# Three moves in the issue order of one tuned kernel: a gate step, a block's first sums, and one half's outputs

## The chip, the cores and the metric

The kernel runs on one core of a Trainium2 chip. The time is device time of one execution in microseconds (us), given as the median of several runs; lower is better. The core has TensorE (PE, matrix products; its weight loads are listed as PEld), VectorE (DVE), ScalarE (ACT), GpSimd (POOL) and SyncE (SP, which issues the transfers).

## The reference

Attention with a window and a few sink positions over 2 x 8 heads of 768 positions, then a mixture of 8 experts, then a feed-forward layer with a squared ReLU:

```python
x = attention(q, k, v)                      # 1536 tokens x 512
P = exp(x @ w_gate - max)                   # 1536 x 8
for _ in range(8):
    P /= P.sum(1) + 1e-9
    P /= P.sum(0) + 1e-9
    P *= N / E
for e in range(8):
    out += P[:, e] * (relu(out_of_attention @ w1[e]) @ w2[e])
h = relu(out @ w_in); result = (h * h) @ w_out
```

All of it is asked for in fp32. The kernel splits every operand of a product into a high and a low part (names that end in h and l) and adds three products: high by high, high by low, low by high.

## The kernel before

**Chunks.** The experts' weights are cut into 16 chunks of 512 hidden columns (c = 0 to 15, two for an expert), the last layer into four (c = 16 to 19). Each chunk has a first product (x by w1 to hidden units h) and a second (h by w2, added up in `acc`). The 1536 tokens are handled as three blocks of 512: blocks 0 and 1 together, and the third block (number 2) alone.

**Fast chunks.** `is_fast` (c = 2 to 15 and 17 to 19) computes first products with a Strassen-like scheme of seven products p1 to p7 on quarters of the operands (`fast`, line 818). Each pi is six matmuls on TensorE (`products`), and an ei behind it takes its result out of PSUM and adds it up on VectorE and ScalarE. It runs with q = 0 on blocks 0 and 1 (512 columns), and with q = 1 on the third block (256 columns), each time for two halves of the hidden units, which I call first half and second half.

**The third block.** With q = 1 a half has only four PSUM banks, a to d, and two groups of products. The first group fills p1 in a, p6 in b, p5 in c, p7 in d (24 matmuls). The second group adds p2 to a, p3 to c, p4 to d (18 matmuls). So p2 may start only when e1 has copied a, p3 only when e5 has read c, p4 only when e7 has read d. The sums hang together: e1 copies a on ACT (tile `txs`), e6 adds it to b (`tu`), e5 adds that to c (the first `tx`), e7 adds that to d (the second `tx`).

The list that `fast` returns is unpacked as `(a, b, *e)` for the first half and `(f, g, *i)` for the second: a and f are the first groups, b and g the second groups, e[0] to e[6] are e1 to e7, and i[0] to i[6] are the same of the second half (I write i1 to i7 for them).

**Outputs.** e2, e3, e4 and e7 hand a result to `to_h` (line 765). For c >= 16 that is a ReLU on ACT (L770), a product on DVE (L771), a copy to `hh` on ACT (L782), and a subtraction to `hl` on DVE (L783). The last two are put in a queue that the next `finish()` issues. For c < 16 it is a ReLU to `hh` on ACT (L767), and `hl` on DVE (L777).

**Order.** Each engine takes its instructions in the order of the program text. `run` goes through `seq`, a list of groups of matmuls, and after group k issues what `plan[k]` holds; `put(m + k, step)` puts a step behind group m + k, where m is the first group after the products of blocks 0 and 1. For 17 <= c the groups from m on are: a, the four second-product groups of block 1 (`second(c, 1)`, 12 matmuls of 512 columns each, at L946, and behind each an addition to `acc` on DVE, L683 or L690), b, f, g, and then `second(c, 0)`. For c < 16 they are the four groups of `second(c, 1)`, a, b, f, g.

**The gate.** `gate` (line 986) computes P. It is a generator: `run` advances it behind those groups whose running number stands in `GATE_AT`. Each of its eight iterations sums rows on DVE and scales (L1024 to L1026), and after a `yield` sums columns by one product with a matrix of ones on TensorE (L1031), whose result DVE uses (L1035 to L1041). The last advance issues the last of these products; it falls into chunk c = 2.

Of the kernel before, what the change touches and what calls it, by code (L numbers as in the profile page):

```python
# [36 lines left out]
FAST, FAST2 = 2, NC1 + 1  # L37
NC = NC1 + NC2
CONV = 3
CONV_AT = (0, 1, 2, 3, 8, 9, 10, 11, 12, 13, 14, 15)  # L40
GATE_AT = (0, 1, 2, 3, 5, 7, 9, 11, 13, 16, 19, 22, 25, 28)
W2_AT = (2, 5, 8, 11)
NB = 512
BIG = 1e30
# [4 lines left out]
class Kernel:  # L49
# [780 lines left out]
    def fast(self, c, half, q):  # L830

        nc = self.nc
        v = {}
        UNITS = {"A11": 0, "A12": 1, "A22": 3, "S2": 4, "S4": 5, "S3": 6, "S1": 7}
        w = NB >> q

        def at(i, f):
            return (c, 2, f, slice(w * i, w * i + w)) if q else (c, i, f, slice(0, w))

        f0, f1 = 2 * half, 2 * half + 1  # L840

        def mul(bank, a, b):
            first = bank not in v
            if first:
                v[bank] = self.mmtile()[:, 0:w]
            self.products(
                v[bank], [(self.weight(c, half, UNITS[a]), self.operand(b, q))], start=first
            )

        def scr(tag):  # L850
            if not q:
                return self.scratch2(tag)
            if (c, tag) not in self.third:
                self.third[c, tag] = self.scratch2(tag)
            return self.third[c, tag][:, w * half : w * half + w]

        def tt(name, a, b, tag=None):
            v[name] = v[b] if tag is None else scr(tag)
            nc.vector.tensor_tensor(out=v[name], in0=v[a], in1=v[b], op=ALU.add)  # L859

        def out(i, f, src):
            c, t, f, s = at(i, f)
            self.to_h(c, t, f, v[src], s)

        def p1():
            mul("a", "A11", "B11")

        def e1():
            if half == 0:
                for t in (2,) if q else (0, 1):  # L870
                    self.h_tiles(c, t)
            v["s"] = self.scratch2("xs" if q else "x0", w)
            nc.scalar.activation(out=v["s"], in_=v["a"], func=AF.Copy)  # L873
            self.finish()

        def p6():
            mul("b", "S2", "T2")

        def e6():
            tt("u", "b", "s", "u")  # L880
            self.finish()

        def p5():
            mul("c", "S1", "T1")

        def e5():
            tt("z", "c", "u", "x0")
            self.finish()

        def p2():  # L890
            mul("a", "A12", "B21")

        def e2():
            self.finish()
            out(0, f0, "a")

        def p7():
            mul("d", "S3", "T3")

        def e7():  # L900
            tt("c22", "d", "z", "x2")
            self.finish()
            out(1, f1, "c22")

        def p3():
            mul("c", "S4", "B22")

        def e3():
            tt("c12", "c", "u", "x0")
            self.finish()  # L910
            out(1, f0, "c12")

        def p4():
            mul("d", "A22", "T4")

        def e4():
            tt("c21", "d", "u")
            self.finish()
            out(0, f1, "c21")

        def chain(*steps):
            def go():
                for step in steps:
                    step()
            return go

        if q == 0:
            pairs = (p1, e1), (p6, e6), (p5, e5), (p2, e2), (p7, e7), (p3, e3), (p4, e4)
            return [chain(*pair) for pair in pairs]
        return chain(p1, p6, p5, p7), chain(p2, p3, p4), e1, e2, e3, e4, e5, e6, e7  # L930

    def second(self, c, t):
# [394 lines left out]
    def phase_b(self, c0, first, fill):  # L1327
# [44 lines left out]
        def run(seq, plan):  # L1372

            for k, g in enumerate(seq):
                g()
                for step in plan.get(k, ()):
                    step()
                if next(groups) in GATE_AT:
                    next(gate, None)
# [5 lines left out]
        for c in range(c0, NC):  # L1385
            if c == 2:
                self.steps = conv
            plan = {}

            def put(k, *step):  # L1390
                plan.setdefault(k, []).append(partial(*step))

            off = 0
            if not low:
                run([self.plain(c, 1, 0), *rest], {})
                low = first.close() or True
                self.w2p = self.pool(left, "w2" + n)
                self.tp = self.pool(left, "T" + n)
                self.cp, self.T = self.pool(left, "c" + n), {}
                seq = [self.plain(c, t, f) for t in (1, 0) for f in range(KD)][1:]  # L1400
            elif self.is_fast(c):
                seq = self.fast(c, 0, 0) + self.fast(c, 1, 0)
            else:
                seq = [self.plain(c, t, f) for t in (1, 0) for f in range(KD)]
            for k in range(4):
                put(W2_AT[k] if self.is_fast(c) else k, self.part_w2, c, k)
            if c == NC1:
                x = [self.x2(2, kc) for kc in range(KD)]
                seq = sum(([s, *x[k : k + 1]] for k, s in enumerate(seq)), [])
            m = len(seq)  # L1410
            if self.is_fast(c):
                (a, b, *e), (f, g, *i) = (self.fast(c, half, 1) for half in range(2))
                if c < FAST2:
                    seq += self.second(c, 1) + [a, b, f, g]
                else:
                    seq += [a] + self.second(c, 1) + [b, f, g]
                for k, step in (
                    (4, e[0]), (4, e[5]), (4, e[4]), (4, e[6]),
                    (6, i[0]), (6, e[1]), (6, e[2]), (6, i[5]), (6, i[4]), (6, e[3]), (6, i[6]),
                    (7, i[1]), (7, i[2]), (7, i[3]),  # L1420
                ):
                    put(m + k, step)
            else:
                seq = seq + self.second(c, 1) + [self.plain(c, 2, f) for f in range(KD)]
            if c == NC1 - 1:
                x = [self.x2(t, kc) for t in (1, 0) for kc in range(KD)]
                seq += sum(
                    ([s, x[k]] for k, s in enumerate(self.second(c, 0) + self.second(c, 2))), []
                )
                wide = lambda k: m + k if k < 8 else m + 2 * k - 8  # L1430
            else:
                seq += self.second(c, 0) + self.second(c, 2)
                wide = lambda k: m + k
            if c in (FAST - 1, FAST2 - 1):
                t = self.sums(0)
                for k in range(13):
                    put(k if c < FAST else min(2 * k, k + 5), next, t, None)
                t = self.sums(1)
                for k in range(13):
                    put(m + 8 + k // 2, next, t, None)  # L1440
            if c + 1 < NC:
                if self.is_fast(c + 1):
                    for half in range(2):
                        for k in range(2):
                            put(wide(2 * half + k), self.unit_sums, c + 1, half, k)
                            put(wide(6 + 2 * half + k), self.units, c + 1, half, 3, k)
                for half in range(2):
                    for k in range(2):
                        put(wide(10 + 3 * half + k), self.units, c + 1, half, 0, k)
            if c > 1:  # L1450
                for k in CONV_AT:
                    put(wide(k), next, conv, None)
                    put(wide(k), next, conv, None)
            run(seq, plan)
# [94 lines left out]
```

## Time and profile before

| | us |
|---|---|
| median of 3 runs | 1413.39 |
| the three runs | 1411.85, 1413.39, 1413.79 |
| the profiled execution's own time | 1413.57 |
| its span, first to last instruction | 1411.7 |
| TensorE busy | 1386.1 |
| VectorE busy | 976.4 |
| POOL busy, ACT busy | 537.3, 471.9 |

The page gives each engine's busy time and share of the span; the list of waits says which engine waited for whom; the timeline gives one row for an instruction (start, duration, engine, source line, operation, output and inputs, shape, and in square brackets how long the engine sat idle before it and what ended that). Matmul rows are pipelined: from one to the next the start moves by less than the duration in the row, so steps are taken from start to start. A line such as L859 is the line of a helper (`tt` of `fast`), so the place is told by the time.

### The profile page before, as it was taken

Reading aid. Unit: us, or ns where it says so; the run is one execution under the profiler, and the core shown is the slowest. Engines: PE = TensorE matmul, PEld = TensorE weight load, DVE = VectorE, ACT = ScalarE, POOL = GpSimd, SP = SyncE. Lnnn points to the kernel's source line nnn. Section 1 sums busy time; section 2 is a strip of 40 time slices with the busy share of each in tenths; the row PEclk is TensorE's granted clock in tenths of the full one; section 3 lists DMA queues with packets and bytes.
Section 4 is the critical chain, followed back from the end, with each engine's and each line's share of the span. In section 5 each row is a group of like instructions: output and inputs, shape, how many; then the busy total and the mean of one; then the engine's idle time right before and its main releaser. Section 6 shows DMA issues by size and latency. Waiting matters only on the chain.

```text
span 1411.7 us, 19345 instructions
## 1 busy us (share of the span) xinstructions
PE 1386.1 (98%) x7225; PEld 1179.8 (84%) x7225; DVE 976.4 (69%) x1932; ACT 471.9 (33%) x1065; POOL 537.3 (38%) x485
## 2 busy tenths in 40 slices
PE   8999999999999999999999999999999999999997
PEld 6888888788888888888888888888888888878786
DVE  7889638888777777777767777765454468846563
ACT  8767423322222222222222222222232243423231
POOL 7534226543442334344233434423342037523210
PEclk9999999999999999999999999999999999999999
DMA  4322110123223232322323232230111010110101
GB/s 161 100 79 88 46 40 30 60 67 105 82 90 105 75 105 68 105 83 90 105 75 105 68 105 83 90 105 31 60 46 60 30 47 27 63 61 30 45 31 63
DMA packets 61148, 102.55 MB, mean 73 GB/s; under 512 B 3956, under 2 KB 43252, under 8 KB 60788
## 3 DMA queue, kind: packets, MB, share of 16 engines
q1 hardware_dynamic: 61040, 101.22, 22.5%
q8 instruction: 59, 0.97, 0.3%
q14 instruction: 45, 0.37, 0.1%
q10 hardware_dynamic: 4, 0.00, 0.0%
HBM read 89.67 MB, written 11.53 MB: 72 GB/s over the span
## 4 chain that ended last, share of the span: by engine, by line
PE 76%; DVE 1%; ACT 0%; issue 0%; ACTq 0%; DVEq 0%
PE mm L946 41%; PE mm L799 35%; PE mm L963 0%; DVE tx L859 0%; ACT hh L782 0%; DVE tu L859 0%; DVE hl L783 0%; DVE acc L690 0%; DVE tx L771 0%; ACT tx L770 0%; DVE tu L771 0%; ACT txs L873 0%; DVE mm L771 0%; DVE acc L686 0%; DVE raw L615 0%
## 5 line engine op out<-in xcount | busy, mean ns | idle before, releaser
L946 PE MATMUL mm<-w2h,hh 128*128 128x512 f32 (+1 forms) x916 | 357.4, 390 | 0.0
L946 PE MATMUL mm<-w2l,hh 128*128 128x512 f32 (+1 forms) x916 | 356.3, 389 | 0.0
L946 PE MATMUL mm<-w2h,hl 128*128 128x512 f32 (+1 forms) x916 | 355.9, 389 | 0.0
L519 POOL TENSOR_TENSOR w2l<-raw,w2h 128x512 fp32r<-128x512 f32 x76 | 118.4, 1557 | 372.1 <-ACT w2h L518 370.1
L690 DVE SCALAR_TENSOR_TENSOR acc<-mm,P,acc 128x512 f32<-128x512 f32 x168 | 125.7, 748 | 137.2 <-PE mm L946 136.0
L946 PEld LDWEIGHTS mm<-w2h,hl 128*128 128x128 f32 x916 | 172.3, 188 | 36.0
L946 PEld LDWEIGHTS mm<-w2h,hh 128*128 128x128 f32 x916 | 172.4, 188 | 34.6
L946 PEld LDWEIGHTS mm<-w2l,hh 128*128 128x128 f32 x916 | 172.4, 188 | 34.4
L562 POOL TENSOR_TENSOR raw<-raw 128x256 f32<-128x256 f32 x136 | 125.7, 928 | 9.1 <-DMA raw<-w 1.0
L519 POOL TENSOR_TENSOR s0l<-raw,s0h 128x512 fp32r<-128x512 f32 (+1 forms) x36 | 45.6, 1266 | 202.5 <-ACT s0h L518 186.8
L767 ACT ACTIVATE hh<-tx 128x512 fp32r<-128x512 f32 (+1 forms) x112 | 58.9, 526 | 90.9 <-DVE tx L859 90.4
L859 DVE TENSOR_TENSOR tx<-mm,tu 128x512 f32<-128x512 f32 (+1 forms) x136 | 75.5, 555 | 17.5 <-PE mm L799 13.6
L859 DVE TENSOR_TENSOR tx<-mm,tx 128x512 f32<-128x512 f32 (+1 forms) x68 | 37.7, 555 | 58.7 <-PE mm L799 57.3
L777 DVE SCALAR_TENSOR_TENSOR hl<-tx,hh 128x512 fp32r<-128x512 f32 (+1 forms) x112 | 69.9, 624 | 7.6 <-ACT hh L767 7.6
L873 ACT ACTIVATE tx<-mm 128x512 f32<-128x512 f32 x34 | 20.4, 599 | 161.3 <-PE mm L799 159.4
L683 DVE TENSOR_TENSOR acc<-mm,acc 128x512 f32<-128x512 f32 (+1 forms) x49 | 33.2, 677 | 58.2 <-PE mm L946 58.1
L873 ACT ACTIVATE txs<-mm 128x256 f32<-128x256 f32 x34 | 13.0, 383 | 173.9 <-PE mm L799 173.9
L767 ACT ACTIVATE hh<-mm 128x512 fp32r<-128x512 f32 (+1 forms) x68 | 34.3, 505 | 102.0 <-PE mm L799 102.0
L519 POOL TENSOR_TENSOR a0l<-raw,a0h 128x512 fp32r<-128x512 f32 (+1 forms) x38 | 43.0, 1149 | 51.8 <-ACT a0h L518 51.8
L519 POOL TENSOR_TENSOR a1l<-raw,a1h 128x512 fp32r<-128x512 f32 (+1 forms) x38 | 40.4, 1084 | 53.3 <-ACT a1h L518 53.3
L799 PE MATMUL mm<-xl,a1h 128*128 128x512 f32 (+1 forms) x172 | 60.3, 350 | 0.0
L799 PE MATMUL mm<-xl,a0h 128*128 128x512 f32 (+1 forms) x172 | 59.8, 348 | 0.0
(276 smaller groups left out, 3409.3 us busy)
## 6 DMA issues: line engine op xcount, KB each, us to landing
raw<-w SPq DMA_DIRECT2D x110, 512.0 KB, 3.6
raw<-win SPq DMA_DIRECT2D x16, 512.0 KB, 4.0
w<-m SPq DMA_DIRECT2D x32, 256.0 KB, 4.5
raw<-wout SPq DMA_DIRECT2D x16, 512.0 KB, 4.1
raw<-qkv SPq DMA_DIRECT2D x8, 624.0 KB, 3.9
raw<-qkv SPq DMA_DIRECT2D x7, 464.0 KB, 3.4
out<-acc SPq DMA_DIRECT2D x11, 256.0 KB, 2.0
wraw<-w SPq DMA_DIRECT2D x2, 1024.0 KB, 5.9
```

Source lines behind the costliest of these rows:

```text
L519: self.nc.gpsimd.tensor_tensor(out=lo, in0=src, in1=hi.bitcast(F32), op=ALU.subtract)
L562: self.nc.gpsimd.tensor_tensor(out=o, in0=x, in1=y, op=op)
L683: nc.vector.tensor_tensor(out=a, in0=ps, in1=a, op=ALU.add)
L690: nc.vector.scalar_tensor_tensor(out=a, in0=ps, scalar=self.P[:, ti, e : e + 1], in1=a, op0=ALU.mult, op1=ALU.add)
L767: nc.scalar.activation(out=hh, in_=src, func=AF.Relu)
L777: nc.vector.scalar_tensor_tensor(out=hl, in0=src, scalar=0.0, in1=hh.bitcast(F32), op0=ALU.max, op1=ALU.subtract,)
L799: self.nc.tensor.matmul(out=ps, lhsT=w[:, kc], rhs=x[:, kc], start=start and k == 0, stop=(k == n - 1), skip_group_check=True,)
L859: nc.vector.tensor_tensor(out=v[name], in0=v[a], in1=v[b], op=ALU.add)
L873: nc.scalar.activation(out=v["s"], in_=v["a"], func=AF.Copy)
L946: self.nc.tensor.matmul(out=ps[:, d], lhsT=x[:, f, s], rhs=w[:, f, d], start=(n == 0), stop=(n == 11),)
```

## The change

The table of the gate has 30 in place of 28 as its last entry. Of the third block's steps, e1, e6 and e5 stand behind group m + 2 in place of m + 4 where c >= 17; e2 and e3 stand behind group b (m + 5) in place of behind f (m + 6); behind f, e4 stands last. The tile for the third block's h is made in e7 in place of e1.

```diff
-GATE_AT = (0, 1, 2, 3, 5, 7, 9, 11, 13, 16, 19, 22, 25, 28)
+GATE_AT = (0, 1, 2, 3, 5, 7, 9, 11, 13, 16, 19, 22, 25, 30)
...
         def e1():
-            if half == 0:
-                for t in (2,) if q else (0, 1):
+            if half == q == 0:
+                for t in (0, 1):
                     self.h_tiles(c, t)
...
         def e7():
             tt("c22", "d", "z", "x2")
+            if half == 0 and q:
+                self.h_tiles(c, 2)
             self.finish()
             out(1, f1, "c22")
...
+                early = 4 if c < FAST2 else 2
                 for k, step in (
-                    (4, e[0]), (4, e[5]), (4, e[4]), (4, e[6]),
-                    (6, i[0]), (6, e[1]), (6, e[2]), (6, i[5]), (6, i[4]), (6, e[3]), (6, i[6]),
+                    (early, e[0]), (early, e[5]), (early, e[4]), (4, e[6]), (5, e[1]), (5, e[2]),
+                    (6, i[0]), (6, i[5]), (6, i[4]), (6, i[6]), (6, e[3]),
                     (7, i[1]), (7, i[2]), (7, i[3]),
                 ):
                     put(m + k, step)
```

**The gate's last product, on TensorE, in chunk c = 2.** The names `mm_` are PSUM tiles; the products are the first half's p6 (T0, s0), p5 (x, s0), p2 (x, a0) and p7 (T0, s0). Before:

```order
L799 MATMUL mm_3321<-T0h_2760,s0h_3072 128x512
L799 MATMUL mm_3321<-T0h_2760,s0l_3073 128x512
L1031 MATMUL mm_3330<-P_84,ones_2508 128x117
L799 MATMUL mm_3335<-xl_82,s0h_3072 128x512
L799 MATMUL mm_3335<-xh_81,s0h_3072 128x512
```

Now, from the middle of p2 on:

```order
L799 MATMUL mm_3308<-xl_82,a0h_3179 128x512
L799 MATMUL mm_3308<-xh_81,a0h_3179 128x512
L799 MATMUL mm_3308<-xh_81,a0l_3180 128x512
L1033 MATMUL mm_3350<-P_84,ones_2508 128x117
L799 MATMUL mm_3355<-T0l_2761,s0h_3072 128x512
L799 MATMUL mm_3355<-T0h_2760,s0h_3072 128x512
```

The product with the ones stood between p6 and p5; now p5 and p2, twelve matmuls, stand ahead of it, and p7 behind it.

**The third block of chunk c = 17, on VectorE.** `acc` rows are the additions behind the groups of `second(c, 1)`; mm_11257, 11264, 11271, 11278 are the first half's banks a, b, c, d. Before, from the last of the four additions to the end of e3's output (i5 follows):

```order
L683 TENSOR_TENSOR acc_83<-mm_11337,acc_83 128x512
L859 TENSOR_TENSOR tu_11355<-mm_11264,txs_11353 128x256
L859 TENSOR_TENSOR tx0_11357<-mm_11271,tu_11355 128x256
L859 TENSOR_TENSOR tx2_11359<-mm_11278,tx0_11357 128x256
L771 SCALAR_TENSOR_TENSOR tx2_11359<-tx2_11359,tx1_11361 128x256
L783 TENSOR_TENSOR hl_11352<-tx2_11359,hh_11351 128x256
L771 SCALAR_TENSOR_TENSOR mm_11257<-mm_11257,tx1_11414 128x256
L859 TENSOR_TENSOR tx0_11357<-mm_11271,tu_11355 128x256
L783 TENSOR_TENSOR hl_11352<-mm_11257,hh_11351 128x256
L771 SCALAR_TENSOR_TENSOR tx0_11357<-tx0_11357,tx1_11420 128x256
L859 TENSOR_TENSOR tu_11355<-mm_11389,txs_11410 128x256
L783 TENSOR_TENSOR hl_11352<-tx0_11357,hh_11351 128x256
```

Now, the same stretch in two pieces, first the sums around the additions:

```order
L683 TENSOR_TENSOR acc_83<-mm_11305,acc_83 128x512
L859 TENSOR_TENSOR tu_11321<-mm_11264,txs_11319 128x256
L859 TENSOR_TENSOR tx0_11323<-mm_11271,tu_11321 128x256
L683 TENSOR_TENSOR acc_83<-mm_11327,acc_83 128x512
L683 TENSOR_TENSOR acc_83<-mm_11343,acc_83 128x512
L859 TENSOR_TENSOR tx2_11357<-mm_11278,tx0_11323 128x256
```

and then from the output of e3 on:

```order
L771 SCALAR_TENSOR_TENSOR tx0_11323<-tx0_11323,tx1_11390 128x256
L783 TENSOR_TENSOR hl_11360<-tx0_11323,hh_11359 128x256
L859 TENSOR_TENSOR tu_11321<-mm_11400,txs_11421 128x256
L859 TENSOR_TENSOR tx0_11323<-mm_11407,tu_11321 128x256
L859 TENSOR_TENSOR tx2_11357<-mm_11414,tx0_11323 128x256
```

e6 and e5 moved ahead of two additions; e7 stands behind the fourth addition, where e6 stood. i6, i5 and i7 (banks 11400, 11407, 11414) follow each other, behind the whole of e3's output.

**The same place on ScalarE.** `txs` is the copy of bank a (e1 and i1), `tx1` a ReLU, `hh` a copy of an output. Before:

```order
L873 ACTIVATE txs_11353<-mm_11257 128x256
L770 ACTIVATE tx1_11361<-tx2_11359 128x256
L873 ACTIVATE txs_11410<-mm_11382 128x256
L782 ACTIVATE hh_11351<-tx2_11359 128x256
L770 ACTIVATE tx1_11414<-mm_11257 128x256
L782 ACTIVATE hh_11351<-mm_11257 128x256
L770 ACTIVATE tx1_11420<-tx0_11357 128x256
L782 ACTIVATE hh_11351<-tx0_11357 128x256
```

Now:

```order
L873 ACTIVATE txs_11319<-mm_11257 128x256
L770 ACTIVATE tx1_11361<-tx2_11357 128x256
L782 ACTIVATE hh_11359<-tx2_11357 128x256
L770 ACTIVATE tx1_11384<-mm_11257 128x256
L782 ACTIVATE hh_11359<-mm_11257 128x256
L770 ACTIVATE tx1_11390<-tx0_11323 128x256
L873 ACTIVATE txs_11421<-mm_11393 128x256
L782 ACTIVATE hh_11359<-tx0_11323 128x256
```

The second half's copy of bank a, second `txs`, stood ahead of all `hh` copies of the first half; now it stands behind those of e7 and e2 and the ReLU of e3.

## Rows read from the trace of the kernel before

**Rows 1.** The page, part 1: busy time, share, instructions.

```profile
PE 1386.1 (98%) x7225; PEld 1179.8 (84%) x7225; DVE 976.4 (69%) x1932; ACT 471.9 (33%) x1065; POOL 537.3 (38%) x485
```

**Rows 2.** Waits of TensorE, longest first: us in total, times, longest us.

```profile
PE mm L799 <- DVE tx L859: 9.1, 10, 1.3
```

**Rows 3.** Timeline of TensorE around the gate's last product.

```profile
270.13 0.39 PE L799 MATMUL mm<-T0h,s0h 128*128 128x512 f32 x1
270.36 0.39 PE L799 MATMUL mm<-T0h,s0l 128*128 128x512 f32 x1
272.52 0.45 PE L1031 MATMUL mm<-P,ones 128*128 128x117 f32 x2 [1.77 <-DVE P L1026]
272.73 0.48 PE L799 MATMUL mm<-xl,s0h 128*128 128x512 f32 x1
```

**Rows 4.** Timeline of VectorE, the last scaling of P.

```profile
271.73 0.64 DVE L1026 TENSOR_TENSOR P<-P,rs 128x96 f32<-128x96 f32 x1
```

**Rows 5.** Timeline of TensorE, third block of chunk c = 17, groups b, f, g.

```profile
1240.34 0.28 PE L799 MATMUL mm<-xl,a0h 128*128 128x256 f32 x1
...
1242.08 0.39 PE L799 MATMUL mm<-xl,s0h 128*128 128x256 f32 x1 [0.86 <-DVE tx L859]
...
1246.49 0.28 PE L799 MATMUL mm<-xl,a1h 128*128 128x256 f32 x1
...
1248.68 0.39 PE L799 MATMUL mm<-xl,s1h 128*128 128x256 f32 x1 [1.30 <-DVE tx L859]
...
1250.31 0.39 PE L799 MATMUL mm<-T1l,a1h 128*128 128x256 f32 x1 [0.66 <-DVE tx L859]
...
1251.13 0.39 PE L946 MATMUL mm<-w2h,hh 128*128 128x512 f32 x1
```

**Rows 6.** Timeline of VectorE in the same stretch.

```profile
1240.54 0.69 DVE L683 TENSOR_TENSOR acc<-mm,acc 128x512 f32<-128x512 f32 x1 [2.03 <-PE mm L946]
1241.15 0.41 DVE L859 TENSOR_TENSOR tu<-mm,txs 128x256 f32<-128x256 f32 x1
1241.60 0.42 DVE L859 TENSOR_TENSOR tx<-mm,tu 128x256 f32<-128x256 f32 x1
1242.06 0.42 DVE L859 TENSOR_TENSOR tx<-mm,tx 128x256 f32<-128x256 f32 x1
1243.02 0.43 DVE L771 SCALAR_TENSOR_TENSOR tx<-tx,tx 128x256 f32<-128x256 f32 x1 [0.54 <-ACT tx L770]
1245.32 0.43 DVE L783 TENSOR_TENSOR hl<-tx,hh 128x256 fp32r<-128x256 f32 x1 [1.86 <-ACT hh L782]
...
1247.86 0.42 DVE L783 TENSOR_TENSOR hl<-tx,hh 128x256 fp32r<-128x256 f32 x1
1248.20 0.42 DVE L859 TENSOR_TENSOR tx<-mm,tu 128x256 f32<-128x256 f32 x1
```

**Rows 7.** Timeline of ScalarE in the same stretch.

```profile
1242.57 0.42 ACT L770 ACTIVATE tx<-tx 128x256 f32<-128x256 f32 x1 [9.33 <-DVE tx L859]
1244.60 0.39 ACT L873 ACTIVATE txs<-mm 128x256 f32<-128x256 f32 x1 [1.60 <-PE mm L799]
1244.88 0.41 ACT L782 ACTIVATE hh<-tx 128x256 fp32r<-128x256 f32 x1
```

**Rows 8.** TensorE by stretches, chunk c = 18: length, busy us, granted clock, DMA.

```profile
1316.00:1318.00 2.00, 1.94 (x8) 0.54 0.00 0
```

**Rows 9.** Timeline of TensorE there, p4 of the second half on.

```profile
1316.06 0.53 PE L799 MATMUL mm<-T1l,a1h 128*128 128x256 f32 x1 [0.66 <-DVE tx L859]
...
1317.46 0.63 PE L946 MATMUL mm<-w2h,hh 128*128 128x512 f32 x1
...
1319.82 0.39 PE L946 MATMUL mm<-w2h,hh 128*128 128x512 f32 x1
```

**Rows 10.** Chunk c = 5, third block: ScalarE's second `txs`, TensorE's p2 of the second half.

```profile
492.24 0.39 ACT L873 ACTIVATE txs<-mm 128x256 f32<-128x256 f32 x1 [1.83 <-PE mm L799]
...
494.14 0.28 PE L799 MATMUL mm<-xl,a1h 128*128 128x256 f32 x1
```

## Prediction

> **What bounds the kernel now.** I read the page first: TensorE is busy for 1386.1 us of a span of 1411.7 us [rows 1], so only some 25 us are open to a change that leaves every product in place, and a wait of another engine counts only where TensorE ends up waiting for it. The list of TensorE's waits comes next. Its largest line is DVE tx L859, 9.1 us in ten waits [rows 2], that is, the third block's sums e5, e7, i5 and i7. The timeline then shows where they are. In chunk c = 17 TensorE goes through b, f and g, 60 matmuls, from 1240.34 to 1251.13, and sits idle for 0.86, 1.30 and 0.66 us before p3 of the first half, p3 of the second and p4 of the second [rows 5]. Chunks 18 and 19 show the same three waits; [rows 9] has the third one of chunk 18. Three times 2.82 is 8.46 us, and the tenth wait, some 0.6 us, is in chunk 2. The one other wait in the reach of the change is the gate's, 1.77 us in chunk 2 [rows 3].
>
> The tail behind the last product holds no step that the change touches, and TensorE's work behind each of these places is a solid row of products. So what is saved at them arrives at the end, as long as nothing later is late; that is a rival below. All terms are taken from the profiled execution, 1413.57 us, which lies 0.18 us above the median of 1413.39.
>
> **The gate's product.** TensorE starts p6's last matmul at 270.36 and would go on at 270.59 (the step of a 512-column matmul is 0.23 us, 270.13 to 270.36); it starts the product with the ones at 272.52, when P is there [rows 3]. P's scaling runs from 271.73 to 272.37 on DVE [rows 4] and doesn't depend on p5 or p2. With twelve matmuls ahead, 12 x 0.23 = 2.8 us, the product comes up at about 273.3, 0.9 us after P is ready. So the whole idle time goes: 272.52 - 270.59 = **1.93 us**. What is late next: e5, which p3 needs, has its place on DVE right behind e6 and now ahead of the gate's last three small steps; e7 stands behind these. p3 is not due before p7's six matmuls, 1.4 us, have passed, and e7 not before p4, another 1.4 us, so I count nothing against it. Bounds: 0, if P were later than the products take, and 2.1, if the restart of the row of matmuls (its first steps are longer, below) goes with it.
>
> **The first half's sums (b's wait).** Before, DVE takes the addition of the fourth group at 1240.54, e6 at 1241.15, e5 at 1241.60, e7 at 1242.06, and p3 starts 0.48 us after e5, at 1242.08 [rows 5, 6]. Banks b and c are long full by then; only the place in DVE's order makes them late. Now e6 and e5 stand behind the second addition, and DVE has 2.03 us of idle time ahead of such an addition [rows 6], which holds their two steps of 0.45. Queued behind them are two additions, which nobody waits for soon. e7 takes e6's old place, 1241.15, so p4 can start at 1241.15 + 0.48 = 1241.63. A 256-column matmul takes a step of 0.12: from 1242.08 to 1246.49 there are 36, the first longer by 0.10 for it follows a wait (below), so 4.31 / 36 [rows 5]. So p3 is due at 1240.34 + 6 x 0.12 = 1241.06 and p4 at 1241.78. Both are free, p4 with 0.15 to spare. If that margin fails it costs about 0.1. A step across a wait also lengthens the following one from 0.12 to 0.22, so a wait costs its excess plus 0.10: from 1250.31 to 1251.13 six matmuls take 0.82, not 0.72 [rows 5]. In all b saves 1.02 + 0.10 a block.
>
> **The second half's sums (g's waits).** This is the term that needs a sum, for here the change puts work ahead of the critical step. The block without waits takes 60 x 0.12 = 7.20; it takes 10.79, so 3.59 is lost. Now p3 of the second half (matmul 49 of 60) is due at 1240.34 + 48 x 0.12 = 1246.10. Its release is i5, which stands on DVE behind i6, and i6 behind the whole outputs of e7, e2 and e3. Their steps wait for ACT and back, in a chain:
> e7 at 1241.15; ReLU + 0.51 (1242.06 to 1242.57); product + 0.45 (1242.57 to 1243.02); `hh` copy, taken as another DVE-to-ACT step, + 0.51; `hl` + 0.44 (1244.88 to 1245.32) [rows 6, 7]. That is 1243.06, against 1245.32 before, where DVE sat idle for 1.86 because the copy stood on ACT behind the second half's `txs`, which had to wait until 1244.60 for f's p1 [rows 7].
> From there to the last `hl` of e3 it took 2.54 (1245.32 to 1247.86), so 1245.60. Then + 0.34 to i6 (1247.86 to 1248.20 is such a step between independent rows), + 0.45 to i5, + 0.48 to TensorE: **1246.87**. i1's copy stands behind e3's ReLU now, and its bank is full soon after 1243.3, so it is in time for i6.
> p3 then waits 1246.87 - 1246.10 = 0.77, and costs 0.87 with its restart. i7 follows i5 by 0.46 and releases p4 at 1247.33, before p3's six matmuls (0.82) are through; the third wait is gone. The block takes 7.20 + 0.87 = 8.07, and saves 10.79 - 8.07 = 2.72. Three blocks: **8.16 us**. Bounds: 3 x 1.12 = 3.4, if only b's wait goes (1.02 + 0.10) and g waits as before; 3 x 3.59 = 10.8, if no wait is left. I take 8.16, since every hop of the chain is a row of the same block.
>
> **The clock.** In chunk 18, right after the waits of g, the granted clock of the stretch 1316 to 1318 is 0.54, the lower of its two levels for most of it [rows 8]; p4's six matmuls take 1.40 in place of 0.82, and the next six 2.36 (1317.46 to 1319.82) in place of 6 x 0.23 = 1.38 [rows 9]. That is 0.58 + 0.98, or **1.56 us**. It hits one of three blocks with equal waits, so it isn't certain to happen, and with a single wait of 0.77 in place of 1.02, 1.47 and 0.81 TensorE is idle much less before it. I take it as gone; the bounds are 0 and 1.56.
>
> **Free of cost.** The h tile made in e7 issues no instruction; its first write, the `hh` copy of e7, waits for the fourth group's last matmul, which is over at 1240.5, two us before. In chunks 2 to 15 (14 third blocks) only outputs and i-steps trade places: in chunk 5 `txs` starts at 492.24 and p2 needs it at 494.14 [rows 10], and with 1.5 us to spare after its 0.39 three short output steps ahead of it change nothing. The tenth wait, in chunk 2, is e5 behind a backlog of DVE; its place there stays, so I leave the 0.6. No DMA moves and the POOL and SP orders stay.
>
> **Sum:** 1413.57 - 1.93 - 8.16 - 1.56 = 1401.92, so **1401.9 us**.
>
> **Rivals.**
> *The clock falls anyway*: 1401.9 + 1.56 = 1403.5. For it: two blocks with the same waits kept the clock, so waits alone don't decide it. The Trainium skill, page "TensorE: Matmul & The Clock Gate", section "Why this matters for your kernels", ties the loss of the clock to one idle gap between bursts that is longer than any of these; by that rule the waits aren't the cause, and removing them wouldn't remove the fall. Against it: in the trace it begins right at the third wait. Chance 0.17.
> *The wait moves, and g waits as before*: the chain of outputs ahead of i6 is longer than summed, by 1.6 us or more, for instance because each ACT step also waits for the buffer of the ReLU. Then each block saves 1.12: 1413.57 - 1.93 - 3.4 - 1.56 = 1406.7. Against it: before, the same steps ran in 2.54 us. Chance 0.08.
> *No wait left in the block*: the hops overlap better, 1401.9 - 3 x 0.87 = 1399.3. It needs i5 0.77 earlier. Chance 0.06.
> *The gate's wait only moves* (P still not there): 1403.8. Chance 0.04.
> *The gain does not reach the end*: weights of the next chunk come from POOL and DMA, and TensorE, earlier by 2.7, could wait for them instead. About 1412, where only a microsecond or two is kept. Against it: the list of waits has no weight of these chunks in it, and loads start when buffers are read, so they move along. Chance 0.06.
> *Slower*: in the 14 blocks of chunks 2 to 15 the copy i1 now stands behind three outputs on ACT. If each block's p2 waited, it would cost more than the 11.7 gained from 0.83 us a block on, and pass 0.2% slower at 1.03. The copy would have to start 1.5 + 1.03 = 2.5 us later than now, at 494.8. At 1.1 a block: 1401.9 + 15.4 = 1417.3. Against it: e3's inputs are there before f's p1 ends. Chance 0.03.
>
> **How the numbers follow.** The forecast has 0.56. The range takes in the forecast with about a third of a microsecond of slip in each block, the fallen clock, the moved gate and the block without waits: **1399.2 to 1404.6**, 0.83 in all; the long chain, the gain that is lost and the slower case lie outside. A measurement of this kernel tells 0.2% (2.8 us) from no change: faster by more 0.91, within 0.06, slower 0.03.
>
> **What would show it.** In the changed profile: no idle time before the product with the ones; the line of DVE tx L859 down from 9.1 to about 2.5 us, in four waits (three of 0.5 to 0.8 before p3 of the second half and one in chunk 2); none before p3 of the first half; third blocks of chunks 17 to 19 of about 8.1 us; the granted clock at 1.00 through them. I am wrong if p3 of the second half still waits more than 1.3 us, if waits for POOL or a transfer appear behind a block, or if chunks 2 to 15 show waits for ACT `txs`.

## The result, and the profile after

The changed kernel takes **1401.29 us** (median of 4 runs, 1400.83 to 1402.07) against 1413.45 us before (median of 4, 1411.85 to 1413.79). The ratio is 0.9917, with a 95% interval of 0.9900 to 0.9934. The forecast was 1401.9 us in a range of 1399.2 to 1404.6. The profiled execution took 1400.87 us, with a span of 1399.1 us. Measured a second time beside other kernels, the changed kernel gave 1401.54 us and a ratio of 0.9918 (0.9900 to 0.9936).

The page of the changed kernel, part 1, answers [rows 1]:

```profile
PE 1380.9 (99%) x7225; PEld 1176.2 (84%) x7225; DVE 981.6 (70%) x1932; ACT 473.2 (34%) x1065; POOL 536.3 (38%) x485
```

No instruction was added or taken away: TensorE has its 7225 matmuls as before. The list of TensorE's waits (us in total, times, longest) answers [rows 2]:

```profile
PE mm L799 <- DVE tx L859: 3.0, 4, 1.0
```

The line of the third block's sums fell from 9.1 us in ten waits to 3.0 in four. The line of the gate is no longer in the list, and no line for a transfer of weights has come into it. Its lines for POOL, 0.2 us each, are of the attention, as the one of 0.3 us before.

**The gate.** TensorE around the product with the ones, to be held against [rows 3]:

```profile
271.15 0.39 PE L799 MATMUL mm<-xh,a0h 128*128 128x512 f32 x1
271.38 0.39 PE L799 MATMUL mm<-xh,a0l 128*128 128x512 f32 x1
271.61 0.37 PE L1033 MATMUL mm<-P,ones 128*128 128x117 f32 x2
271.75 0.48 PE L799 MATMUL mm<-T0l,s0h 128*128 128x512 f32 x1
```

and VectorE's scaling of P, to be held against [rows 4]:

```profile
270.04 0.68 DVE L1028 TENSOR_TENSOR P<-P,rs 128x96 f32<-128x96 f32 x1
```

P is done at 270.04 + 0.68 = 270.72, and the product comes at its turn at 271.61, with 0.89 us to spare. (The lines behind line 902 have moved by two: L1033 is the former L1031.)

**The third block of chunk 17.** TensorE, to be held against [rows 5]: p2, p3 and p4 of the first half, the last matmul of p2 of the second half, its p3 and p4, and the first matmul behind the block:

```profile
1236.67 0.28 PE L799 MATMUL mm<-xl,a0h 128*128 128x256 f32 x1
...
1237.38 0.28 PE L799 MATMUL mm<-xl,s0h 128*128 128x256 f32 x1
...
1238.10 0.28 PE L799 MATMUL mm<-T1l,a0h 128*128 128x256 f32 x1
...
1242.30 0.28 PE L799 MATMUL mm<-xh,a1l 128*128 128x256 f32 x1
1243.29 0.39 PE L799 MATMUL mm<-xl,s1h 128*128 128x256 f32 x1 [0.71 <-DVE tx L859]
...
1244.11 0.28 PE L799 MATMUL mm<-T1l,a1h 128*128 128x256 f32 x1
...
1244.83 0.40 PE L948 MATMUL mm<-w2h,hh 128*128 128x512 f32 x1
```

Of the three waits one is left, before p3 of the second half. The block takes 1244.83 - 1236.67 = 8.16 us, where it took 10.79. Chunk 18 shows the same (0.70 idle). In chunk 19 the wait is longer:

```profile
1369.87 0.39 PE L799 MATMUL mm<-xl,s1h 128*128 128x256 f32 x1 [0.99 <-DVE tx L859]
```

VectorE in chunk 17, to be held against [rows 6], from the fourth addition to i7:

```profile
1236.87 0.69 DVE L683 TENSOR_TENSOR acc<-mm,acc 128x512 f32<-128x512 f32 x1 [2.03 <-PE mm L948]
1237.48 0.41 DVE L859 TENSOR_TENSOR tx<-mm,tx 128x256 f32<-128x256 f32 x1
1238.44 0.42 DVE L771 SCALAR_TENSOR_TENSOR tx<-tx,tx 128x256 f32<-128x256 f32 x1 [0.54 <-ACT tx L770]
1239.40 0.43 DVE L783 TENSOR_TENSOR hl<-tx,hh 128x256 fp32r<-128x256 f32 x1 [0.54 <-ACT hh L782]
...
1241.04 0.42 DVE L771 SCALAR_TENSOR_TENSOR tx<-tx,tx 128x256 f32<-128x256 f32 x1
1241.94 0.42 DVE L783 TENSOR_TENSOR hl<-tx,hh 128x256 fp32r<-128x256 f32 x1 [0.48 <-ACT hh L782]
1242.29 0.42 DVE L859 TENSOR_TENSOR tu<-mm,txs 128x256 f32<-128x256 f32 x1
1242.81 0.43 DVE L859 TENSOR_TENSOR tx<-mm,tu 128x256 f32<-128x256 f32 x1
1243.34 0.42 DVE L859 TENSOR_TENSOR tx<-mm,tx 128x256 f32<-128x256 f32 x1
```

From top to bottom: the addition, e7, e7's product and `hl`, e3's product and `hl`, then i6, i5 and i7. Behind the addition VectorE sits idle three times in it, each time for an answer of ScalarE. The idle time of 1.86 us ahead of the first `hl` in [rows 6] has become 0.54.

**Where the time went.** Matmul by matmul, in program order, the starts in the changed profile can be set against those of the profile before. The lead of the changed kernel grows at these places and, behind 80 us, nowhere else by more than 0.15 us:

| place | lead at its end | gained there |
|---|---|---|
| up to 80 us, in the attention | 1.70 | 1.70 |
| the gate, chunk 2 | 3.70 | 2.00 |
| third block, chunk 17 | 6.30 | 2.61 |
| third block, chunk 18, with the clock | 10.48 | 4.18 |
| third block, chunk 19 | 12.81 | 2.34 |

At the end of the program 12.70 us are left between the two executions (1413.57 and 1400.87). The first line isn't the change's. Its code is the same in both kernels, but the profile of before shows a stretch of low granted clock there (TensorE by stretches: length, busy us and count, granted clock, share of DMA, GB/s):

```profile
64.00:68.00 4.00, 4.00 (x21) 0.64 0.13 48
```

The same stretch of the changed kernel:

```profile
64.00:68.00 4.00, 4.00 (x31) 1.00 0.19 66
```

From 59 to 75 us the lead grows by 2.1 us; 0.4 had been lost ahead of it.

### The profile page after: what moved, and what is told of

It is laid out like the page before. It is cut to its first block, busy times and chain, and to the rows that moved or that the text cites. A ratio compares the mean times of both kernels' runs of the same rounds, so it can differ in the third digit from the quotient of the medians.

```text
span 1399.1 us, 19364 instructions
## 1 busy us (share of the span) xinstructions
PE 1380.9 (99%) x7225; PEld 1176.2 (84%) x7225; DVE 981.6 (70%) x1932; ACT 473.2 (34%) x1065; POOL 536.3 (38%) x485
## 4 chain that ended last, share of the span: by engine, by line
PE 77%; DVE 1%; ACT 0%; issue 0%; DVEq 0%; ACTq 0%
PE mm L948 41%; PE mm L799 35%; PE mm L965 0%; ACT hh L782 0%; DVE hl L783 0%; DVE tx L859 0%; DVE tx L771 0%; DVE acc L683 0%; ACT tx L770 0%; DVE acc L690 0%; DVE tu L859 0%; DVE mm L771 0%; DVE acc L686 0%; DVE raw L615 0%; DVE raw L602 0%
```

## The experiments

The theory on record has three parts: the gate's wait of 1.93 us goes whole; of the third block's waits only one of 0.77 us stays, because i6 stands behind the whole of e3's output; and the fall of the clock in chunk 18 goes with the waits. The rivals that the result leaves are these. Either the parts are not what they seem (a larger gain from one, a smaller from another), or the wait that stays has another cause than e3's output, or the clock falls by itself and has nothing to do with the waits. Of each kernel below only the edit to the kernel before is shown, where nothing else is said.

### The gate alone, and one product less

```diff
-GATE_AT = (0, 1, 2, 3, 5, 7, 9, 11, 13, 16, 19, 22, 25, 28)
+GATE_AT = (0, 1, 2, 3, 5, 7, 9, 11, 13, 16, 19, 22, 25, 30)
```

> The kernel before with the gate's last advance two products later and nothing else. My theory: only the idle time before the product with the ones goes, 1.93 us, plus 0.05 to 0.1 of its restart; so 2.0 us under the kernel before (about 1411.4), the nine waits of the third blocks of chunks 17 to 19 unchanged at 8.5 us. Rival (the wait only moves): the product with the ones, or e5 or e7 behind it, waits instead, and less than 0.7 us is gained.

Measured: 1411.49 us (1408.01 to 1414.9, 11 runs) against 1413.35 (15 runs), ratio 0.9988 (0.9978 to 0.9997). In its trace the lead grows at the gate by 2.00 us, and the ten waits of the third blocks are there unchanged (9.1 us). So this term is right alone, too; the medians differ by 1.86.

How much of the margin the second product gives was asked with the changed kernel and the gate's product placed one product earlier:

```diff
-GATE_AT = (0, 1, 2, 3, 5, 7, 9, 11, 13, 16, 19, 22, 25, 30)
+GATE_AT = (0, 1, 2, 3, 5, 7, 9, 11, 13, 16, 19, 22, 25, 29)
```

> The changed kernel with the gate's last entry at 29, so that one product (six matmuls of 0.23 us) and not two moves ahead of the product with the ones. P was ready for TensorE at 272.52 and the product would be due at 270.59 + 6 x 0.23 = 271.97: by my reckoning a wait of about 0.55 us comes back and the time is about 0.6 us above the changed kernel's, some 1401.9. If P were ready earlier than the trace says, the wait is 0 and 30 was one more than needed.

Measured: 1402.09 us, one run. TensorE there, the last two products ahead of the one with the ones:

```profile
270.21 0.39 PE L799 MATMUL mm<-xh,s0h 128*128 128x512 f32 x1
270.43 0.39 PE L799 MATMUL mm<-xh,s0l 128*128 128x512 f32 x1
271.19 0.48 PE L1033 MATMUL mm<-P,ones 128*128 128x117 f32 x2 [0.37 <-DVE P L1028]
```

It was due at 270.43 + 0.23 = 270.66 and came at 271.19, 0.53 us late, where 0.55 was expected; with the longer steps behind it this kernel falls 0.64 us behind the changed one at this place. Two products are the right number: one is half a microsecond short, and two leave 0.89.

### The first half's sums alone

```diff
+                early = 4 if c < FAST2 else 2
                 for k, step in (
-                    (4, e[0]), (4, e[5]), (4, e[4]), (4, e[6]),
+                    (early, e[0]), (early, e[5]), (early, e[4]), (4, e[6]),
```

(with the tile for h made in e7, as in the change)

> The kernel before with e1, e6 and e5 of chunks 17 to 19 behind the second group, the order of the outputs and the gate as before. My theory: p3 of the first half no longer waits (1.02 + 0.10 a block), and g waits as before (1.46 and 0.81, each + 0.10), since the second half's copy of bank a still stands on ScalarE ahead of the first half's output copies; 3 x 1.12 = 3.4 us under the kernel before, about 1410.0. Rival (the early sums bring the whole gain, the order of the outputs is beside the point): about 8.2 us under it, about 1405.2.

Measured: 1408.24 us (1406.46 to 1409.01, 5 runs), ratio 0.9966 (0.9952 to 0.9979). The trace shows the wait of 0.86 us in group b gone and those of 1.30 and 0.66 us as they were, seven in all with the one in chunk 2:

```profile
PE mm L799 <- DVE tx L859: 6.5, 7, 1.3
```

The fall of the sum from 9.1 us is the three waits of 0.86; the lead grows by 1.11 us in chunks 17 and 19, where 1.12 was reckoned. Three times 1.11 is 3.33, but the median fell by 5.1, to 1.8 us under the 1410.0 expected. The waits that were to go went and the others stayed; the rest goes with the clock: this profile has neither the fall in chunk 18, 1.56 us against the profile of before, nor the one in the attention. For the runs without a profile this is not shown. I come back to it.

### The new order of the outputs alone

```diff
-                    (4, e[0]), (4, e[5]), (4, e[4]), (4, e[6]),
-                    (6, i[0]), (6, e[1]), (6, e[2]), (6, i[5]), (6, i[4]), (6, e[3]), (6, i[6]),
+                    (4, e[0]), (4, e[5]), (4, e[4]), (4, e[6]), (5, e[1]), (5, e[2]),
+                    (6, i[0]), (6, i[5]), (6, i[4]), (6, i[6]), (6, e[3]),
```

(again with the tile for h made in e7)

> The kernel before with the outputs e2 and e3 around group b's end and e4 last, the first sums behind the fourth group and the gate as before. My theory: p3 of the first half waits as before (1.02), p3 of the second half waits 0.65 in place of 1.46, and p4 of the second half no longer waits; 1.73 a block, so 5.2 us under the kernel before, about 1408.2. Rival (the order only matters once the sums are early): less than 1.5 us.

Measured: 1406.22 us (1405.14 to 1408.42, 5 runs), ratio 0.9955 (0.9941 to 0.9968). The list of TensorE's waits has this line:

```profile
PE mm L799 <- DVE tx L859: 5.0, 7, 0.9
```

Each block keeps the wait of 0.86 us in b; p3 of the second half waits less, as in chunk 17,

```profile
1246.04 0.39 PE L799 MATMUL mm<-xl,s1h 128*128 128x256 f32 x1 [0.51 <-DVE tx L859]
```

and p4 of the second half doesn't wait. The blocks gain 1.72, 1.70 and 1.43 us, the clock's share taken out, where the sum has 2.72 - 1.12 = 1.60 for this part. That is 4.85 in all; the median fell by 7.1, and here too the rest goes with the clock, since this profile has neither of the two falls of before. The two parts add up nearly: 1.11 + 1.72 = 2.83 in chunk 17, against 2.61 together. The 0.2 between them can be followed. Both at once bring TensorE to p3 of the second half 1.12 us earlier in the block, but e7, which starts the chain of outputs, only 0.91 (from 1242.06 to 1241.15 in the times of before), since it stands behind the fourth addition.

### e3's output out of the way

If the wait that stays is there because e3's queued `hh` and `hl` stand ahead of i6 and i5, then letting i7 issue them, and not i1, takes it away. This edit is to the changed kernel, in `fast`; e1, e6 and e5 call `rest()` where they called `self.finish()`:

```diff
+        def rest():
+            if not (half and q and c >= FAST2):
+                self.finish()
```

> The changed kernel, with one more move in chunks 17 to 19: i1, i6 and i5 no longer issue the queued rest of e3's output (hh on ScalarE, hl on VectorE); it is issued by i7, so on VectorE i6, i5 and i7 stand ahead of that hl. My theory (the wait left before p3 of the second half is the chain of e7's, e2's and e3's outputs ahead of i6): i6 comes 0.9 us earlier, i5 releases p3 at about its due time, and the wait of 0.7 to 1.0 goes to 0.1 or less in each of three blocks; 2.6 us under the changed kernel, about 1398.7. Rival (f's products set i5, not the outputs): the wait stays above 0.5, and the time within 0.8 us of the changed kernel.

Measured: **1397.79 us** (1397.62 to 1398.71, 4 runs), ratio to the kernel before 0.9894 (0.9879 to 0.9909). Of VectorE's chain in chunk 17, from e3's product on, this is left:

```profile
1240.81 0.43 DVE L771 SCALAR_TENSOR_TENSOR tx<-tx,tx 128x256 f32<-128x256 f32 x1
1241.15 0.42 DVE L859 TENSOR_TENSOR tu<-mm,txs 128x256 f32<-128x256 f32 x1
1241.67 0.42 DVE L859 TENSOR_TENSOR tx<-mm,tu 128x256 f32<-128x256 f32 x1
```

On ScalarE the order stays as it was, i1's copy, e3's `hh`, i7's ReLU; what moves is e3's `hl` on VectorE, behind i7. i6 follows e3's product at once, 0.34 us behind it, where in the changed kernel the idle 0.48 us and e3's `hl` lie between (1242.29 - 1241.04 = 1.25 us). p3 of the second half starts at its turn:

```profile
1242.07 0.28 PE L799 MATMUL mm<-xh,a1l 128*128 128x256 f32 x1
1242.19 0.35 PE L799 MATMUL mm<-xl,s1h 128*128 128x256 f32 x1
```

To have the difference to the changed kernel on one chip, both ran again side by side.

> The changed kernel once more, beside rest_later_pair on one chip: about 1401.3, with its waits of 0.7, 0.7 and 1.0 us in chunks 17 to 19. If waits as short as these don't bring the clock down, its profile has no stretch below 0.9 there; if the clock falls by chance anywhere, one such stretch in three or four blocks is to be expected.

> The kernel of rest_later once more: 3.5 us under the changed kernel, about 1397.8, if the three waits of 0.8, 0.8 and 1.1 with their restarts are the whole difference (2.7) and the clock gives the rest; 1398.6 if only the waits count.

Measured: 1401.54 us (1400.74 to 1402.79) and 1398.51 (1397.18 to 1399.47), 4 runs each, ratios to the same runs of before 0.9918 (0.9900 to 0.9936) and 0.9891 (0.9872 to 0.9909). No run of the changed kernel, in either set, is as short as the longest of the other. In the two traces the lead grows in the three blocks by 0.92, 0.92 and 0.90 us, 2.74 in all; in the attention the best version's profile loses 1.5 us of it to a fall of the clock at 62 to 68 us. The 2.74 is what was expected of the waits (2.7), and the median of 1398.51 is the 1398.6 of the case that only the waits count; the medians differ by 3.0. So the wait that stays comes from e3's `hl`, and VectorE's idle time for its `hh`, in front of i6 and i5, and this is the best version found.

### The clock: chance or the waits?

The kernel before twice more, and the gate alone once more, each for its profile.

> The kernel before, unchanged, for a second look at where its clock falls. If the falls of the granted clock come from the waits of the third blocks, this execution shows at least one stretch below 0.9 within 4 us behind a wait of p4 in chunks 17 to 19, though not necessarily in chunk 18, and its waits are the same 9 us in ten; time about 1413. If the fall in chunk 18 had nothing to do with the waits, the falls lie elsewhere, or there is none.

> The same as before_again_a, a third look at the kernel before: by the waits as the cause, again one fall or more behind the waits of chunks 17 to 19, in whichever block; by chance alone, falls at places without a wait, or none.

> The kernel before with the gate's last entry at 30 alone, a second look. By the waits as the cause of the falls: one or more falls behind the waits of chunks 17 to 19, as its first look showed in chunk 19, and a time of 1408 plus about 1.6 for each fall. Without such a link: no fall there.

Measured: 1413.28, 1414.39 and 1409.05 us, one run each. The first shows the fall in chunk 18 again:

```profile
1316.00:1318.00 2.00, 2.00 (x8) 0.50 0.00 0
1318.00:1320.00 2.00, 2.00 (x7) 0.65 0.00 0
```

The second has none in chunk 18, but one in chunk 17 and one in chunk 19:

```profile
1250.00:1252.00 2.00, 2.00 (x8) 0.52 0.02 4
1252.00:1254.00 2.00, 2.00 (x7) 0.63 0.00 0
1316.00:1318.00 2.00, 1.34 (x10) 1.00 0.00 0
1382.00:1384.00 2.00, 1.53 (x8) 0.80 0.00 0
1384.00:1386.00 2.00, 2.00 (x6) 0.50 0.00 0
1386.00:1388.00 2.00, 2.00 (x9) 0.85 0.00 0
```

The gate alone had none this time, which was expected for the case without a link; one execution can't decide on a fall that comes in some blocks only. Its first profile, which waits at the same places, had one in chunk 19:

```profile
1376.00:1378.00 2.00, 1.24 (x8) 1.00 0.00 0
1378.00:1380.00 2.00, 2.00 (x9) 0.54 0.00 0
1380.00:1382.00 2.00, 2.00 (x7) 0.60 0.00 0
```

Each of these falls begins within a microsecond of the start of p4 of the second half, right behind the third of the block's three waits. In the second profile that start is

```profile
1249.34 0.39 PE L799 MATMUL mm<-T1l,a1h 128*128 128x256 f32 x1 [0.66 <-DVE tx L859]
...
1250.21 0.63 PE L946 MATMUL mm<-w2h,hh 128*128 128x512 f32 x1
1250.64 0.63 PE L946 MATMUL mm<-w2l,hh 128*128 128x512 f32 x1
```

with steps of 0.43 us behind it in place of 0.23. Last, whether the two waits of the second half are enough for it:

> The kernel before with the first half's sums moved and nothing else, a second look: waits of 1.30 and 0.66 us before p3 and p4 of the second half as in the kernel before. If these two set off the clock's falls, about one block in three shows a fall behind the second; if the wait of 0.86 in group b is needed too, none does.

Measured: 1406.4 us, one run; the waits of 1.30 and 0.66 us in all three blocks, and no fall. Over all the profiles taken:

| idle before p3, p3, p4 in each third block | profiles | blocks | falls behind them |
|---|---|---|---|
| 0.86, 1.30, 0.66 (before, the gate alone) | 5 | 15 | 5 |
| 0, 1.30, 0.66 (first sums alone) | 2 | 6 | 0 |
| 0.86, 0.5 to 0.8, 0 (order alone) | 1 | 3 | 0 |
| 0, 0.7 to 1.0, 0 (the change, also with 29) | 3 | 9 | 0 |
| 0, under 0.1, 0 (e3's output later) | 2 | 6 | 0 |

If a fall came by chance in a third of the blocks, whatever their waits and each block for itself, none in 24 blocks would have a probability of (2/3) to the power of 24, well under 1 in 1000. The blocks of one execution need not be independent, though: two of the profiles of before have their falls at the same two places, at 63 and at 1316 us. Counted by profiles, four of the five with the three waits show a fall in a third block and none of the eight others does. If four of 13 were struck at random, all four would be among those five in 5 of 715 cases, under 1 in 100. Between 80 us and chunk 17, moreover, none of the 13 profiles has a fall, though six of them have the gate's single wait of 1.8 us there. So in the profiles the falls in the third blocks hang on the row of three waits. Which of the waits makes it is less sure: the six blocks without the first one had none, but that would happen by chance in (2/3) to the power of 6, some 9 in 100, and they are of two profiles only.

The mean granted clock of a run doesn't say where a fall is, and it also counts the end of the program: in every profile the clock falls once more there, when TensorE has no work left. It was 0.994 to 0.998 in the runs of before, 0.993 to 1.000 with the gate alone, 0.996 to 0.999 with the first sums alone, 0.995 to 1.000 with the order alone, 0.996 to 0.999 in the 8 runs of the changed kernel, and 0.998 to 1.000 in the 8 of the best version. So the clock is higher without the waits on the whole, but not in each run. The first profile of before, with two falls ahead of the end, has 0.996; a run of the changed kernel (1402.79 us) has that, too, and one with the order alone (1408.42 us) has 0.995. These have no profile, so falls in them, in the third blocks or elsewhere, are not ruled out. With the gate alone the 11 runs go from 1408.01 us at 0.999 to 1414.9 us at 0.993, so the clock goes with most of what makes one run of the same kernel differ from another.

## Why the prediction was right

**The gate: right.** Forecast 1.93 us, measured 2.00; the 0.07 is the restart that the sum left out and the bounds held. The margin was put at 0.9 us and is 0.89. What was named as late next, e5 and e7 behind the small steps of the gate, brings no wait.

**The first half's sums: right.** Forecast 1.12 us a block, measured 1.11. p4's margin, put at 0.15 us, is 1238.10 - (1237.48 + 0.48) = 0.14.

**The second half's sums: right in the mechanism, 0.1 us short in two blocks and 0.4 in the third.** In the times of the changed kernel (p2 at 1236.67, 3.67 earlier) the chain of the forecast reads, with the measured start behind each step: e7 1237.48 (1237.48), its `hl` 1239.39 (1239.40), e3's `hl` 1241.93 (1241.94), i6 1242.27 (1242.29), i5 1242.72 (1242.81), p3 1243.20 (1243.29). The step that was mis-sized is the one from i6 to i5: I took 0.45 from e6 and e5 and it is 0.52. So a block takes 8.16 us in place of 8.07. In chunk 19 the wait is 0.28 us longer still, for a reason that the forecast had no row for. ScalarE, from e2's `hh` to e3's ReLU there:

```profile
1366.50 0.39 ACT L782 ACTIVATE hh<-mm 128x256 fp32r<-128x256 f32 x1 [0.56 <-DVE mm L771]
1367.16 0.42 ACT L770 ACTIVATE tx<-tx 128x256 f32<-128x256 f32 x1 [0.27 <-ACT hh L782]
```

and the same two steps in chunk 18:

```profile
1303.34 0.38 ACT L782 ACTIVATE hh<-mm 128x256 fp32r<-128x256 f32 x1 [0.56 <-DVE mm L771]
1303.72 0.42 ACT L770 ACTIVATE tx<-tx 128x256 f32<-128x256 f32 x1
```

In all the blocks gain 2.61 + 2.62 + 2.34 = 7.57 us (chunk 18 with 1.56 for the clock taken out), where the sum had 8.16.

**The clock: taken as gone, and in the profiles it is gone.** The changed kernel's three profiles (one of them with the gate's entry at 29) show 1.00 in the third blocks of chunks 17 to 19. In the first of them TensorE has there

```profile
1236.00:1246.00 10.00, 9.29 (x70) 1.00 0.01 2
1299.00:1309.00 10.00, 9.30 (x70) 1.00 0.00 0
1362.00:1372.00 10.00, 9.01 (x68) 1.00 0.14 55
```

But the sum priced it from one profile, as one fall of 1.56 us in chunk 18. Three profiles of before have four falls in nine blocks, 1.3 for an execution, some 2.1 us, and not always in the same chunk. The rival that it falls anyway is not borne out by the table above; for runs without a profile it stays open. The rule of the Trainium skill that stood for that rival (page "TensorE: Matmul & The Clock Gate", section "Why this matters for your kernels", one idle gap longer than any in these blocks) doesn't foresee these falls: five blocks lost the clock behind idle times of 0.86, 1.30 and 0.66 us, with work between them. Here the measurement decides: in these traces several short waits in a row cost the clock too.

**Why the forecast is so near.** Two errors of opposite sign lie in it. The blocks gained 0.6 us less than summed. And the profile of before held a second fall of the clock, at 62 to 68 us in the attention, that the sum didn't touch and that the profile after doesn't have; some 1.7 us of the 12.7 between the two executions were gained up to there. It isn't tied to either version: of 13 profiles, three show it, two of the kernel before and one of the best version. What the sum was about measured 2.00 + 7.57 + 1.56 = 11.13 us, against 11.65 in the forecast. In the two profiled executions the 1.7 us of the attention more than make up for the difference, and this part of the nearness is luck.

**The other rivals.** That g waits as before is refuted by the one wait of 0.71 us in place of 1.30 and 0.66. That no wait is left would have needed i5 0.77 us earlier, and the kernel with e3's output out of the way shows what that takes. That the gain doesn't reach the end is refuted by the lead: 12.81 us behind chunk 19, and still 12.70 at the end. The slower case hung on i1's copy in chunks 2 to 15; in chunk 5 of the changed kernel ScalarE has

```profile
488.55 0.38 ACT L873 ACTIVATE txs<-mm 128x256 f32<-128x256 f32 x1 [0.58 <-PE mm L799]
```

which still waits for TensorE's p1, just as in [rows 10]. The three outputs ahead of it are through by then, and p2 starts at 490.45, with 1.5 us to spare. The wait in chunk 2, left in the sum as it was, is 0.60 us as before.

## What to carry to other kernels

Write out the chain of small steps between engines hop by hop, from rows of the same block, and set its end against the moment at which the waiting engine would be due; here it held to 0.1 us from e7 to p3, where looking at the shares of busy time would have said nothing. When a wait stays behind an edit, look what stands ahead of its releaser in that engine's order without being needed by it: moving e3's `hl` behind i7 gave another 3 us. And compare several profiles of the same kernel before a term is priced from one of them: a fall of the clock is there in one execution and elsewhere in the next.

## What the runs showed of the hardware that I had not expected

- The granted clock falls to its lower level (0.50 of full speed, 1.2 GHz) behind rows of short waits: in 5 of 15 blocks with idle times of 0.86, 1.30 and 0.66 us, each time at a price of about 1.6 us, and in none of the 24 other blocks. A single wait of 1.8 us, at the gate in six profiles, was followed by none.
- The clock also falls at places that no edit touched: at 62 to 68 us in three of 13 profiles, and in one (the changed kernel with the gate's entry at 29) at 24 to 30 us. Why they come in some executions only stays open.
- A sum on VectorE that needs the one just ahead of it starts 0.45 us after that one in the first half (e6 to e5, 1241.15 to 1241.60 before) and 0.52 in the second (i6 to i5, 1242.29 to 1242.81 after), with the same shape and operation. The first is the same in the changed kernel and with the order alone, the second with the order alone and with e3's output later (1241.15 to 1241.67). Why was not tried.
- The hitch of 0.27 us on ScalarE in chunk 19 comes at the same step in the changed kernel, with the order alone (0.27) and with e3's output later (0.28). In each of the three traces a packet of a queue that loads instructions starts 1.5 to 1.7 us ahead of the late ReLU, and in chunk 18 of the changed kernel there is none in the five microseconds ahead of it. But in chunk 17 of the same three traces such a packet starts 1.6 to 1.7 us ahead of the same step, and there the step is on time. So a packet alone doesn't make it late, and the cause stays open.
